# The first heads of an attention stage: rows of maxima on ScalarE's queue, copies and loads in another order, and twelve transposes by transpose mode

## The chip, the cores and the metric

The kernel runs on one core of a Trainium2 chip. The metric is the device time of one execution, in microseconds. The kernel before was timed three times: 921.12, 921.53 and 918.25 us, median 921.12 us.

The core has five engines with instruction queues of their own: TensorE (PE; its weight loads, PEld, run beside it), VectorE (DVE), ScalarE (ACT), GpSimd (POOL) and SyncE (SP). Each works through its instructions in the order in which they are written, and waits where an instruction needs something that is not there yet. A DMA is issued by an engine's queue too: by SP nearly everywhere here, by ACT for the first weights of the last stage and, after the change, for a few small rows.

## The reference

Three stages follow each other: causal attention with a decay, a gated feed-forward network, and eight experts to which tokens are assigned greedily.

```python
# attention: 4 batches x 8 heads = 32 heads, 576 positions, 64 columns
scores = (q @ k.T) / sqrt(64) + cum[:, None] - cum[None, :]   # cum = cumsum(log(clip(f)))
scores = where(causal, -1e9, scores); scores -= max(scores, -1)
attn = exp(scores); attn /= sum(attn) + 1e-9;  x = attn @ v
# gated network on 2304 tokens x 512
x = (sigmoid(x @ w_gate) * (x @ w_val)) @ w_out
# 8 experts, 288 tokens each: the greatest logits of x @ w_gate2 first, until an expert is full
out[mask_e] = maximum(x[mask_e] @ w1[e], 0) @ w2[e]
```

## The kernel before

**What a head needs.** `attention` works on 32 heads, two to a pair. For head h:

- `load(p)` brings q and k of a pair (576 KB) into one of three buffers `raw`; `decays(p)` adds two rows (the decay) to it; `load_v(p)` brings v (`vf`, 330 KB, three buffers).
- `prep(h)` (ACT, L126) rounds q and k into one of four tiles `P1` (`P` in the trace). Row 66 of that tile holds the row of maxima; rows 64 to 66 start as ones, and 64 zero columns stand ahead.
- `copies(h)`: two DMAs of 144 KB from `P1` into the tile `p2` (`p` in the trace). `prep2(h)` (POOL, L139 and L140) fills the other halves of it with the remainders of the rounding.
- `maxpass(h)`: TensorE makes the rounded scores (six matmuls, into `p1b` and `pb`), DVE takes the maxima of the 128-row blocks (L159).
- `mrows(h)`: TensorE turns the maxima into rows (`pb<-identr,mx`), ACT copies them (L185); `mstore(h)` sends them by DMA (2.5 KB, L188) into row 66 of `P1`.
- `scores(h)`: twelve matmuls; the first of them (`py<-P`) needs row 66, the others `p2` too. ACT takes the exponentials (L208), and POOL cuts the diagonal blocks (`affine_select`, L212).
- `av(h)`: TensorE multiplies by `vf` (ten jobs into `pv`), ACT copies the result (L238), and `store` sends a pair's result to DRAM.

**The order.** Nothing is scheduled by a program: the order of each engine is that of the calls. In the loop over h, TensorE does `scores(h)`, then `av(h-1)` with `mrows(h+2)` and `maxpass(h+3)` set between its jobs, so each row of maxima is made about two heads before it is used. The first heads are written out apart: there is not yet a head to lay the work beside, and `warm(n)` fills gaps with n matmuls whose results nobody reads. In the loop, head 1 has `rows(2)`, `prep(4)` and `maxpass(3)`, and head 2 has `mrows(3)` at the end of `scores(2)`, `maxpass(4)`, `rows(4)`, and then `maxpass(5)`.

**Before the loop.** The decay (`ck`) is made by DVE and ACT from f (L111 to L116), and goes by DMA into rows 64 and 65 of `P1` (L130); only then can `maxpass(0)` start. Meanwhile POOL sets the ones and zeros of the four `P1` tiles (L104, L105) and the ones in `raw` (L119).

**Later.** `fill(h)` puts the splitting of the next stage's weights (DMA `mr<-ww`, L406 to L423) beside the heads. After attention come the gated network (`Ffn`), the assignment (`Route`), and `First.turn`: it turns the 288 gathered rows of expert 0 by matmuls with an identity matrix, three for each of four column blocks (L1020), and adds 16 rows that came another way (L1022). The experts turn their rows in the same manner, but with `nc.tensor.transpose` (L1047).

Of the kernel before, what the change touches and what calls it, by code (L numbers as in the profile page):

```python
# [6 lines left out]
F32 = mybir.dt.float32  # L7
# [27 lines left out]
def make_consts(ev, pool, keep):  # L35

    nc = ev.nc

    jp = pool.tile([128, 128], I32, name="jp")
    nc.gpsimd.iota(jp, pattern=[[1, 128]], base=0, channel_multiplier=-1)  # L40
    ev.identb = pool.tile([128, 128], BF16, name="identb")
    nc.vector.tensor_scalar(ev.identb, jp, 0.0, None, op0=OP.is_equal)
    yield
    ev.mq = pool.tile([128, S], BF16, name="mq")
    nc.vector.memset(ev.mq[:, :448], 0.0)
    nc.vector.tensor_scalar(ev.mq[:, 448:], jp, 0.0, BIG, op0=OP.is_gt, op1=OP.mult)
    ev.identr = pool.tile([128, 128], F32R, name="identr")
    nc.vector.tensor_scalar(ev.identr, jp, 0.0, None, op0=OP.is_equal)
    yield
    ev.ident = keep.tile([128, 128], F32, name="ident")  # L50
    nc.vector.tensor_scalar(ev.ident, jp, 0.0, None, op0=OP.is_equal)
    ev.fold = keep.tile([16, E], F32, name="fold")
    nc.vector.tensor_tensor(ev.fold, ev.ident[:16, 0:8], ev.ident[:16, 8:16], op=OP.add)
    yield
# [2 lines left out]

AT = (2, 4)
FIRST = {2: -3, 4: -2, 5: -1}
WARM = (19, 4, 6, 2)  # L60
KT = [(0, 0, 0, 1024), (0, 128, 128, 0), (0, 256, 256, 512), (0, 384, 384, 832), (64, 448, 512, 448)]


def attention(ev, qkT, vr, f, xs, rec, ckd, fill):
# [4 lines left out]
    with ExitStack() as ctx:  # L69
# [11 lines left out]
        def load(p):  # L81
            r = RAW3[p % 3]
            nc.sync.dma_start(r[0:64], qkT[2 * p:2 * p + 2].rearrange("h d s -> d h s"))
            RAW[2 * p], RAW[2 * p + 1] = r[:, 0], r[:, 1]

        def decays(p):

            nc.sync.dma_start(RAW3[p % 3][64:66, :, S:], ckd[:, 2 * p:2 * p + 2])
# [11 lines left out]
        nc.scalar.activation(idle, zero, AF.Ln, bias=1.0)  # L100
        next(consts)
        P1 = [st.tile([67, 64 + 2 * S], F32R, name=f"P1_{i}") for i in range(4)]
        for t in P1:
            nc.gpsimd.memset(t[64:67].bitcast(F32), 1.0)  # L104
            nc.gpsimd.memset(t[0:64, 0:64].bitcast(F32), 0.0)  # L105

        junk = st.tile([128, 1600], BF16, name="mj")
        JT = (0, 64, 256, 576, 1024)
        ck = st.tile([NHEAD, 2, S], F32R, name="ck")
        next(consts)  # L110
        nc.vector.tensor_scalar(ft, ft, 1e-4, 1.0, op0=OP.max, op1=OP.min)  # L111
        nc.scalar.activation(ft, ft, AF.Ln)
        cum = st.tile([NHEAD, S], F32, name="cum")
        nc.vector.tensor_tensor_scan(cum, ft, zero.to_broadcast([NHEAD, S]), 0.0, op0=OP.add, op1=OP.add)
        nc.vector.tensor_scalar(ck[:, 0], cum, -8.0, None, op0=OP.mult)
        nc.vector.scalar_tensor_tensor(ck[:, 1], cum, -8.0, ck[:, 0], op0=OP.mult, op1=OP.subtract)  # L116

        def ones(p):
            nc.gpsimd.memset(RAW3[p][64:66, :, :S], 1.0)  # L119
# [4 lines left out]
        def prep(h, n=66):  # L124
            p1 = P1[h % 4]
            nc.scalar.activation(p1[0:n, Q0:], RAW[h][0:n], AF.Copy)  # L126
            P2[h] = wk.tile([128, 2 * S], F32R, name="p2", bufs=4)

        def decay(h):
            nc.sync.dma_start(P1[h % 4][64:66, K0:].bitcast(F32), ck[h:h + 1].bitcast(F32))  # L130

        def copies(h):
            p1, p2 = P1[h % 4], P2[h]
            nc.sync.dma_start(p2[0:64, :S].bitcast(F32), p1[0:64, Q0:K0].bitcast(F32))
            nc.sync.dma_start(p2[64:128, S:].bitcast(F32), p1[0:64, K0:].bitcast(F32))

        def prep2(h, engine=nc.gpsimd):
            r, p1, p2 = RAW.pop(h), P1[h % 4], P2[h]
            engine.tensor_tensor(p2[64:128, :S], r[0:64, :S], p1[0:64, Q0:K0], op=OP.subtract)  # L139
            engine.tensor_tensor(p2[0:64, S:], r[0:64, S:], p1[0:64, K0:], op=OP.subtract)  # L140
# [44 lines left out]
            nc.scalar.activation(MR[h], b[0:5, 0:128], AF.Copy)  # L185

        def mstore(h):
            nc.sync.dma_start(P1[h % 4][66:67, 0:640].bitcast(F32), MR.pop(h))  # L188

        def scores(h, m=None):  # L190
            p1, p2 = P1[h % 4], P2.pop(h)
            y = ps2.tile([128, 1024], F32, name="py")
            x = ps1.tile([128, 512], F32, name="p1b")
            z = ps1.tile([128, 512], F32, name="p1b")

            def sc(out, k0, q0, q1, first=True, last=True):
                mm(out, p1[0:67, K0 + k0:K0 + k0 + 128], p1[0:67, Q0 + q0:Q0 + q1], first, False)
                mm(out, p2[:, S + k0:S + k0 + 128], p2[:, q0:q1], False, last)

            sc(y[:, 256:512], 0, 0, 256)  # L200
            sc(y[:, 512:832], 0, 256, 576)
            sc(x[:, 0:448], 128, 128, 576, last=False)
            sc(x[:, 448:512], 448, 512, 576, False)
            sc(z[:, 0:320], 256, 256, 576, last=False)
            sc(z[:, 320:512], 384, 384, 576, False)
            e = EX[h] = wk.tile([128, 1600], F32, name="e", bufs=3)
            for c0, c1, src in ((1024, 1600, y[:, 256:832]), (0, 512, x), (512, 1024, z)):
                nc.scalar.activation(e[:, c0:c1], src, AF.Exp, scale=0.125)  # L208

            for first, step, n, base in ((0, 512, 3, 0), (448, 384, 2, 64)):  # L210
                t = blocks(e, first, step, n)
                nc.gpsimd.affine_select(out=t, in_=t, pattern=[[-base, n], [1, 128]], compare_op=OP.is_ge, fill=0.0,  # L212
                                        base=base, channel_multiplier=-1)
            if m:
                mrows(m)
# [46 lines left out]
        warm(WARM[0])  # L262
        for h in (0, 1):
            decay(h)
        nc.sync.dma_start(ckd.rearrange("r h s -> h r s"), ck.bitcast(F32))
        for h in (0, 1):
            prep(h, 64)
# [21 lines left out]
        load_v(0)  # L289
        copies(2)  # L290
        decays(2)
        load(2)
        copies(3)
        warm(WARM[3])
        maxpass(2)
        prep2(3)
        ones(2)
        for h in range(1, NHEAD):
            odd = h % 2
            scores(h, 3 if h == 2 else None)  # L300
            if h == 1:
                ones(0)
            if h == 2:
                mstore(3)
                next(consts)

            def rows(r):
                if r < NHEAD:
                    mrows(r)
                    mstore(r)  # L310

            def early():
                rows(h + 2 if h > 1 else 2)
                if h == 1:
                    prep(4)
                    prep2(4)
                elif h + 4 < NHEAD:
                    prep(h + 4)

            def late():  # L320
                if h + 3 < NHEAD:
                    maxpass(h + 3)

            if h == 1:
                av(0, {2: early, 3: lambda: maxpass(3)})
                prep(5)
            elif h == 2:
                av(1, {0: lambda: maxpass(4), 5: early})
                late()
            else:  # L330
                av(h - 1, {AT[0]: early, AT[1]: late})
            if h < NHEAD - 3:
                copies(h + 3)
            if h >= 3 and odd:
                store(h // 2 - 1)
            if h == 1:
                load(3)
                decays(3)
            if not odd and h // 2 + 3 < NPAIR:
                load(h // 2 + 3)  # L340
                decays(h // 2 + 3)
            if odd and h // 2 + 1 < NPAIR:
                load_v(h // 2 + 1)
            for b in range(B - 1):
                step = {2: 0, 4: 1, 5: 2}.get(h - (b + 1) * H)
                if step is not None:
                    recip(b, step)
            if h + 4 < NHEAD:
                prep2(h + 4)
            if h in FIRST:  # L350
                fill(FIRST[h])
            fill(h)
# [640 lines left out]
class First:  # L993
# [19 lines left out]
    def turn(self, x, bank):  # L1013

        nc = self.nc
        for k in range(4):
            ks = slice(k * 128, (k + 1) * 128)
            p = bank()
            for i in range(3):
                nc.tensor.matmul(p[:, i * TT:(i + 1) * TT], self.xg[i][:, ks], self.ev.ident[:TT, :TT], start=i == 0,  # L1020
                                 stop=False, skip_group_check=True)
            nc.tensor.matmul(p[:, :CH], x[:, ks], self.hot[:, :CH], start=False, stop=True, skip_group_check=True)  # L1022
            nc.scalar.activation(self.x[0][:, k], p[:, :CH], AF.Copy)  # L1023
            nc.vector.tensor_tensor(self.x[1][:, k], p[:, :CH], self.x[0][:, k], op=OP.subtract)  # L1024
# [251 lines left out]
```

## Time and profile before

| what | value |
|---|---|
| runs | 918.25, 921.12, 921.53 us |
| profiled execution: its own time | 924.52 us |
| its span, first to last instruction | 922.6 us |
| mean granted TensorE clock, as a share of full speed | 0.987 |
| PE busy | 901.5 us (98%) |
| DVE, ACT, POOL busy | 548.7, 330.7, 459.9 us |
| the chain that ended last | PE 22%, issue 4%, POOL 2% (within the part that was followed back) |

The span of the profile lies 1.92 us under the execution's own time; the rest is start and end. A busy PE is not a PE at its peak: with the granted clock at one half the same matmuls take twice as long and still count as busy. So the rows of the clock are read beside those of the busy time. The attention stage takes about the first 190 us, the gated network goes on to about 600 us, the assignment to about 676 us, and the experts to the end.

### The profile page before, as it was taken

How to read it: one execution, taken by the hardware profiler on the slowest of the kernel's cores; microseconds unless marked ns; L12 is line 12 of the kernel's file. 1: busy time of each engine (PE TensorE's matmuls, PEld its weight loads, DVE VectorE, ACT ScalarE, POOL GpSimd, SP SyncE). 2: the span in 40 equal slices, each digit the busy share in tenths (PEclk: the TensorE clock that was granted, in tenths of full speed). 3: DMA queues.
4: the chain of work that ended last, by engine and by line, in shares of the span. 5: the costliest groups of instructions: out<-in, count | busy, mean ns of one | idle time of the engine just before them, and what ended most of it. 6: DMA issues, size and time to landing. Idle time of an engine off the chain costs nothing. (4 is left out here: it accounts for less than half of the span.)

```text
span 922.6 us, 14053 instructions
## 1 busy us (share of the span) xinstructions
PE 901.5 (98%) x5182; PEld 758.9 (82%) x5182; DVE 548.7 (59%) x1185; ACT 330.7 (36%) x571; POOL 459.9 (50%) x393
## 2 busy tenths in 40 slices
PE   7899999999999999999999999999989999999995
PEld 4677777778788888888888888887789999999995
DVE  5387886818885497988989642535524443444431
ACT  5566667642322211121111222211126444444530
POOL 8678898925565122121222221222138777777741
PEclk9899999999999999999999999999979999999998
DMA  6777999845551203010121210011247666656610
GB/s 142 164 205 213 237 235 235 213 130 170 171 168 64 75 0 92 18 63 13 47 62 26 66 46 1 1 44 46 70 144 233 207 190 193 196 172 210 201 37 26
DMA packets 49016, 111.30 MB, mean 121 GB/s; under 512 B 11346, under 2 KB 11762, under 8 KB 48946
## 3 DMA queue, kind: packets, MB, share of 16 engines
q1 hardware_dynamic: 44786, 98.85, 37.7%
q0 software_dynamic: 3072, 9.44, 3.1%
q10 hardware_dynamic: 1088, 2.10, 0.7%
q8 instruction: 41, 0.67, 0.3%
q14 instruction: 29, 0.24, 0.1%
HBM read 86.12 MB, written 14.71 MB: 109 GB/s over the span
## 5 line engine op out<-in xcount | busy, mean ns | idle before, releaser
L509 POOL TENSOR_TENSOR gl<-sg,gh 128x512 fp32r<-128x512 f32 x36 | 49.7, 1379 | 201.1 <-ACT gh L508 201.1
L985 POOL TENSOR_TENSOR elo<-eraw,ehi 128x1024 fp32r<-128x1024 f32 x45 | 107.9, 2410 | 45.2 <-ACT ehi L983 44.9
L143 PE MATMUL pv<-e,vf 128*65 128x256 f32 (+1 forms) x434 | 106.5, 370 | 0.8 <-DMA vf<-vv 0.8
L502 PE MATMUL gv<-xah,w_hi 128*128 128x512 f32 (+1 forms) x288 | 103.2, 358 | 0.0
L502 PE MATMUL gv<-xal,w_hi 128*128 128x512 f32 (+1 forms) x288 | 102.9, 357 | 0.0
L502 PE MATMUL gv<-xah,w_lo 128*128 128x512 f32 (+1 forms) x288 | 102.8, 357 | 0.0
L542 DVE CUSTOM_DVE_ANT_0 mb<-mb,bc 128x512 f32<-128x512 f32 x96 | 82.2, 856 | 3.3
L542 DVE CUSTOM_DVE_ANT_0 mb<-mr,bc 128x512 f32<-128x512 f32 x96 | 81.9, 853 | 2.8
L508 ACT ACTIVATE gh<-sg 128x512 fp32r<-128x512 f32 x36 | 22.8, 633 | 156.4 <-PE o L521 84.4
L1072 PE MATMUL ey<-hh,ehi 128*128 128x288 f32 x256 | 78.0, 305 | 0.0
L1072 PE MATMUL ey<-hl,ehi 128*128 128x288 f32 x256 | 76.4, 299 | 0.0
L502 PE MATMUL gv<-xbh,w_hi 128*128 128x512 f32 x192 | 76.1, 396 | 0.0
L502 PE MATMUL gv<-xbl,w_hi 128*128 128x512 f32 x192 | 76.1, 396 | 0.0
L502 PE MATMUL gv<-xbh,w_lo 128*128 128x512 f32 x192 | 76.0, 396 | 0.0
L1072 PE MATMUL ey<-hh,elo 128*128 128x288 f32 x256 | 75.7, 296 | 0.0
L143 PEld LDWEIGHTS pv<-e,vf 128*65 128x65 f32 x434 | 50.3, 139 | 25.1 <-issue 15.4
L143 PE MATMUL p1b<-P 66*128 66x192 f32 (+7 forms) x256 | 66.0, 326 | 3.5 <-DMA P<-ck 1.8
L159 DVE CUSTOM_DVE_ANT_0 mj<-p1b,mq 128x192 bf16<-128x192 f32 (+3 forms) x128 | 46.6, 419 | 37.7 <-PE p1b L143 37.7
L1059 PE MATMUL eh<-xeh,ehi 128*128 128x288 f32 x224 | 67.8, 303 | 0.0
L1059 PE MATMUL eh<-xeh,elo 128*128 128x288 f32 x224 | 66.3, 296 | 0.0
L1059 PE MATMUL eh<-xel,ehi 128*128 128x288 f32 x224 | 66.3, 296 | 0.0
L1062 DVE SCALAR_TENSOR_TENSOR hl<-eh,hh 128x288 fp32r<-128x288 f32 x64 | 29.1, 456 | 62.4 <-ACT hh L1061 62.4
(213 smaller groups left out, 2305.7 us busy)
## 6 DMA issues: line engine op xcount, KB each, us to landing
eraw<-w SPq DMA_DIRECT2D x56, 512.0 KB
mr<-ww SPq DMA_DIRECT2D x26, 512.0 KB
raw<-qk SPq DMA_DIRECT2D x16, 576.0 KB
p<-P SPq DMA_DIRECT2D x64, 144.0 KB
vf<-vv SPq DMA_DIRECT2D x16, 330.0 KB
bc<-ww SPq DMA_DIRECT2D x10, 512.0 KB
xs<-xo SPq DMA_DIRECT2D x16, 292.5 KB
x2d<-mr SPq DMA_DIRECT2D x17, 256.0 KB
```

What stands on the lines that cost most here:

```text
L143: nc.tensor.matmul(out, lhsT, rhs, start=start, stop=stop, skip_group_check=True)
L159: nc.vector.tensor_tensor_reduce(out=junk[:, JT[t]:JT[t] + n], in0=src, in1=ev.mq[:, S - n:], op0=OP.add, op1=OP.min, scale=-1.0, scalar=3 ...
L502: nc.tensor.matmul(p[i][:, :m], w_[:, ws], x_[:, k], start=n == 0, stop=n == 11)
L508: nc.scalar.activation(hi, s, AF.Copy)
L509: nc.gpsimd.tensor_tensor(lo, s, hi, op=OP.subtract)
L542: nc.vector.tensor_tensor_reduce(out=junk, in0=a, in1=self.bc[j], op0=OP.mult, op1=OP.add, scale=1.0, scalar=0.0, accum_out=res)
L985: eng.tensor_tensor(lo, r, hi, op=OP.subtract)
L1059: nc.tensor.matmul(p[:, :CH], w_[:, ws], x_[:, k], start=n == 0, stop=n == 11)
L1062: nc.vector.scalar_tensor_tensor(h[1][:, f], p[:, :CH], 0.0, h[0][:, f], op0=OP.max, op1=OP.subtract)
L1072: nc.tensor.matmul(p[:, :CH], w_[:, ws], h_[:, f], start=n == 0, stop=n == 23)
```

## The change

1. `mstore(h)` issues from ACT's queue for h < 6, and from SP's as before for the others.
2. The ones of `P1` are no longer set by POOL: tiles 0 and 1 by ACT (after the logarithm), tiles 2 and 3 by DVE (after `ck`). POOL keeps the zero columns.
3. The loop's first three heads are written anew: `mrows(3)` and `mstore(3)` stand ahead of `scores(2)`; `prep(4)`, `prep(5)` come behind the exponentials of head 2; `copies(4)` and `copies(5)` with them; `maxpass(4)` behind `av(1)`, and `maxpass(6)` and `rows(5)` behind `av(2)`.
4. `load(3)` and `load_v(1)` are issued before the loop, and `load_v` runs one pair further ahead all through; `copies(3)` goes ahead of `load(2)`.
5. The 128x128 identity and the 16x8 fold matrix are made at heads 30 and 31 and not at head 2; `warm` has 20 matmuls and not 19 at the start.
6. In `First.turn` the three matmuls with the identity carry `is_transpose=True`.

```diff
-WARM = (19, 4, 6, 2)
+WARM = (20, 4, 6, 2)
...
         P1 = [st.tile([67, 64 + 2 * S], F32R, name=f"P1_{i}") for i in range(4)]
-        for t in P1:
-            nc.gpsimd.memset(t[64:67].bitcast(F32), 1.0)
-            nc.gpsimd.memset(t[0:64, 0:64].bitcast(F32), 0.0)
...
         nc.scalar.activation(ft, ft, AF.Ln)
+        for t in P1[:2]:
+            nc.scalar.activation(t[64:67], zero[0:3].to_broadcast([3, 64 + 2 * S]), AF.Copy, bias=1.0)
...
+        for t in P1[2:]:
+            nc.vector.memset(t[64:67].bitcast(F32), 1.0)
...
         def mstore(h):
-            nc.sync.dma_start(P1[h % 4][66:67, 0:640].bitcast(F32), MR.pop(h))
+            (nc.scalar if h < 6 else nc.sync).dma_start(P1[h % 4][66:67, 0:640].bitcast(F32), MR.pop(h))
...
         for h in (0, 1):
             decay(h)
+        for t in P1:
+            nc.gpsimd.memset(t[0:64, 0:64].bitcast(F32), 0.0)
...
         decays(2)
+        copies(3)
         load(2)
-        copies(3)
+        load(3)
+        load_v(1)
...
-            scores(h, 3 if h == 2 else None)
-            if h == 1:
-                ones(0)
             if h == 2:
+                mrows(3)
                 mstore(3)
-                next(consts)
+            scores(h)
...
             if h == 1:
-                av(0, {2: early, 3: lambda: maxpass(3)})
-                prep(5)
+                ones(0)
+                decays(3)
+                av(0, {2: lambda: rows(2), 3: lambda: maxpass(3)})
             elif h == 2:
-                av(1, {0: lambda: maxpass(4), 5: early})
+                prep(4)
+                prep2(4)
+                av(1)
+                prep(5)
+                prep2(5)
+                maxpass(4)
+            elif h == 3:
+                av(2, {2: lambda: rows(4), 3: lambda: maxpass(5), 5: lambda: prep(6)})
+                rows(5)
+                prep(7)
                 late()
+                prep2(6)
             else:
                 av(h - 1, {AT[0]: early, AT[1]: late})
-            if h < NHEAD - 3:
+            if h == 2:
+                copies(4)
+                copies(5)
+            elif 2 < h < NHEAD - 3:
                 copies(h + 3)
...
-            if odd and h // 2 + 1 < NPAIR:
-                load_v(h // 2 + 1)
+            if odd and h > 1 and h // 2 + 2 < NPAIR:
+                load_v(h // 2 + 2)
...
                 nc.tensor.matmul(p[:, i * TT:(i + 1) * TT], self.xg[i][:, ks], self.ev.ident[:TT, :TT], start=i == 0,
-                                 stop=False, skip_group_check=True)
+                                 stop=False, is_transpose=True, skip_group_check=True)
```

**Where instructions moved.** Three places, each before and after. The first is ACT's order from the exponentials of head 1 to those of head 3 (`e<-` exponentials, `mr<-pb` copies of rows of maxima, `P_0_116` and `P_1_117` the tiles that heads 4 and 5 use, `xo<-pv` results of `av`). Before:

```order
L208 ACTIVATE e<-py 128x576
L208 ACTIVATE e<-p1b 128x512 x2
L185 ACTIVATE mr<-pb 5x128
L126 ACTIVATE P_0_116<-raw_105 66x1152
L238 ACTIVATE xo<-pv 65x576
L126 ACTIVATE P_1_117<-raw_105 66x1152
L208 ACTIVATE e<-py 128x576
L208 ACTIVATE e<-p1b 128x512 x2
L185 ACTIVATE mr<-pb 5x128 x2
```

and after, over the same piece of work:

```order
L209 ACTIVATE e<-py 128x576
L209 ACTIVATE e<-p1b 128x512 x2
L186 ACTIVATE mr<-pb 5x128
L189 DMA P_2_118<-mr 1x5x128
L239 ACTIVATE xo<-pv 65x576
L186 ACTIVATE mr<-pb 5x128
L189 DMA P_3_119<-mr 1x5x128
L209 ACTIVATE e<-py 128x576
L209 ACTIVATE e<-p1b 128x512 x2
L127 ACTIVATE P_0_116<-raw_105 66x1152
L239 ACTIVATE xo<-pv 65x576
L127 ACTIVATE P_1_117<-raw_105 66x1152
```

Both stores of rows of maxima are now ACT's own, both stand ahead of the exponentials of head 2, and the two `prep` of heads 4 and 5 stand behind them. The second place is TensorE's order from the end of `av(0)` on (`py<-P_2_118` is the first matmul of `scores(2)`, `p1b<-P_0_116` the first of `maxpass(4)`). Before, the last rows of `scores(2)` and what follows:

```order
L143 MATMUL p1b<-P_2_118 128x192
L143 MATMUL p1b<-p_219 128x192
L143 MATMUL pb<-identr,mx 5x128
L143 MATMUL p1b<-P_0_116 128x192
L143 MATMUL p1b<-P_0_116 128x320
L143 MATMUL p1b<-P_0_116 128x448
L143 MATMUL p1b<-P_0_116 128x64
L143 MATMUL pb<-P_0_116 128x256
L143 MATMUL pb<-P_0_116 128x320
L143 MATMUL pv<-e,vf 65x256
```

and after:

```order
L144 MATMUL p1b<-P_2_118 128x192
L144 MATMUL p1b<-p_220 128x192
L144 MATMUL pv<-e,vf 65x256
L144 MATMUL pv<-e,vf 65x320
L144 MATMUL pv<-e,vf 65x128
L144 MATMUL pv<-e,vf 65x320
L144 MATMUL pv<-e,vf 65x192
L144 MATMUL pv<-e,vf 65x64
L144 MATMUL pv<-e,vf 65x320
L144 MATMUL p1b<-P_0_116 128x192
```

The matmuls of `av(1)` now stand between `scores(2)` and `maxpass(4)`, and the row of maxima of head 3 is made before `scores(2)`. The third place is SP's queue from the decay of pair 2 (`raw_105`) on. Before:

```order
L88 DMA raw_105<-ckd 2x2x576
L83 DMA raw_105<-qk 64x2x1152
L134 DMA p_255<-P_3_119 64x576
L135 DMA p_255<-P_3_119 64x576
L188 DMA P_2_118<-mr 1x5x128
L134 DMA p_315<-P_0_116 64x576
L135 DMA p_315<-P_0_116 64x576
L83 DMA raw_103<-qk 64x2x1152
L88 DMA raw_103<-ckd 2x2x576
L92 DMA vf<-vv 128x660
```

and after:

```order
L89 DMA raw_105<-ckd 2x2x576
L135 DMA p_256<-P_3_119 64x576
L136 DMA p_256<-P_3_119 64x576
L84 DMA raw_105<-qk 64x2x1152
L84 DMA raw_103<-qk 64x2x1152
L93 DMA vf<-vv 128x660
L89 DMA raw_103<-ckd 2x2x576
L135 DMA p_367<-P_0_116 64x576
L136 DMA p_367<-P_0_116 64x576
```

The row of maxima of head 2 (`P_2_118<-mr`) no longer stands behind the load of pair 2 and the copies of head 3, and the load of pair 3 and the second `vf` stand ahead of the copies of head 4.

## Rows read from the trace of the kernel before

**Rows 1.** Stretches: start:end, length, busy (x count) by engine, PEclk, DMA share, GB/s.
```profile
30.00:40.00 10.00, 10.00 (x43) 6.84 (x44) 3.58 (x18) 3.84 (x7) 6.00 (x7) 0.71 0.61 134
...
29.00:30.00 1.00, 1.00 (x5) 0.81 (x4) 0.74 (x5) 0.23 (x2) 0.97 (x1) 0.51 0.30 74
```

**Rows 2.** PE in time: start us, us, what [idle before <- releaser].
```profile
22.80 1.27 PE L143 MATMUL pv<-e,vf 128*65 128x192 f32 x5
25.74 0.39 PE L143 MATMUL py<-P 67*128 67x256 f32 x1 [1.67 <-DMA P<-mr]
...
28.66 1.28 PE L143 MATMUL p1b<-P 66*128 66x192 f32 x4 [0.92 <-ACT e L208]
...
36.87 0.28 PE L143 MATMUL py<-P 67*128 67x256 f32 x1
...
39.34 0.46 PE L143 MATMUL pb<-identr,mx 128*5 128x128 f32 x1
...
40.16 0.91 PE L143 MATMUL p1b<-P 66*128 66x192 f32 x4
...
41.24 1.43 PE L143 MATMUL pv<-e,vf 128*65 128x192 f32 x6
42.27 0.52 PE L143 MATMUL py<-P 67*128 67x256 f32 x1
...
47.83 0.52 PE L143 MATMUL py<-P 67*128 67x256 f32 x1
...
50.73 1.16 PE L143 MATMUL pv<-e,vf 128*65 128x256 f32 x4 [0.83 <-DMA vf<-vv]
```

**Rows 3.** SP's queue in time (and PE's weight load that its first store releases).
```profile
13.13 2.97 SPq L188 DMA_DIRECT2D P<-mr  x2
...
15.01 0.19 PEld L143 LDWEIGHTS py<-P 67*128 67x128 f32 x1 [0.30 <-DMA P<-mr]
...
21.62 0.75 SPq L188 DMA_DIRECT2D P<-mr  x1
...
42.99 0.44 SPq L92 DMA_DIRECT2D vf<-vv  x1
```

**Rows 4.** ACT and its queue in time.
```profile
24.84 1.16 ACT L126 ACTIVATE P<-raw 66x1152 fp32r<-66x1152 f32 x1 [3.28 <-DMA raw<-qk]
...
27.49 0.63 ACT L208 ACTIVATE e<-py 128x576 f32<-128x576 f32 x1
28.02 1.07 ACT L208 ACTIVATE e<-p1b 128x512 f32<-128x512 f32 x2
...
685.91 1.98 ACTq L961 DMA_DIRECT2D eraw<-w  x4
```

**Rows 5.** Instructions of a tile (0 to 60) or line: count, ns min/median/max.
```profile
L188 SPq DMA_DIRECT2D P<-mr x9: 700/747/818, 13.1 to 57.9; - x9
...
L406 DVE TENSOR_SCALAR mb<-mr x26: 414/912/2849, 48.5 to 277.2; 128x512 uint32<-128x512 uint32 x26
```

**Rows 6.** The front, all engines in time.
```profile
2.63 1.10 POOL L104 MEMSET P<- 3x1216 f32 x1
2.70 1.34 DVE L111 TENSOR_SCALAR ft<-ft 32x576 f32<-32x576 f32 x1
...
7.83 1.46 SPq L130 DMA_DIRECT2D P<-ck  x2
...
9.84 0.73 PE L143 MATMUL p1b<-P 66*128 66x192 f32 x4 [1.79 <-DMA P<-ck]
```

**Rows 7.** The chain that ended last: start us, us, what.
```profile
680.09 0.64 PE gv L1020 x6
...
681.39 1.23 PE gv L1020 x6
...
702.09 0.25 PE et L1047 x3
```

**Rows 8.** One more stretch, as in Rows 1: the turn of expert 0.
```profile
680.80:691.00 10.20, 9.21 (x35) 7.91 (x34) 2.01 (x5) 2.08 (x5) 2.77 (x3) 0.51 0.59 178
```

More of the change, by code (lines that the diff above doesn't have):

```diff
@@ L51, in make_consts @@
     nc.vector.tensor_scalar(ev.ident, jp, 0.0, None, op0=OP.is_equal)
+    yield
     ev.fold = keep.tile([16, E], F32, name="fold")
@@ L312, in early @@
             def early():
[L313 to L317, printed above, removed]
+                rows(h + 2)
+                if h + 4 < NHEAD:
                     prep(h + 4)
@@ L324, in attention @@
             if h == 1:
-                av(0, {2: early, 3: lambda: maxpass(3)})
-                prep(5)
-            elif h == 2:
-                av(1, {0: lambda: maxpass(4), 5: early})
+                ones(0)
+                decays(3)
+                av(0, {2: lambda: rows(2), 3: lambda: maxpass(3)})
+            elif h == 2:
+                prep(4)
+                prep2(4)
+                av(1)
+                prep(5)
+                prep2(5)
[4 more added lines that the diff above has]
+                prep(7)
                 late()
+                prep2(6)
             else:
                 av(h - 1, {AT[0]: early, AT[1]: late})
-            if h < NHEAD - 3:
+            if h == 2:
+                copies(4)
+                copies(5)
+            elif 2 < h < NHEAD - 3:
                 copies(h + 3)
@@ L335, in attention @@
                 store(h // 2 - 1)
-            if h == 1:
-                load(3)
-                decays(3)
+            if h == 2:
+                load_v(2)
             if not odd and h // 2 + 3 < NPAIR:
@@ L347, in attention @@
                     recip(b, step)
-            if h + 4 < NHEAD:
+            if 2 < h < NHEAD - 4:
                 prep2(h + 4)
+            if h > NHEAD - 3:
+                next(consts)
             if h in FIRST:
```

## The prediction

> **What bounds the kernel now.** I read the stretches first, then TensorE in time, then what released each of its waits. TensorE is busy 98% of the span, so most of the time can only change by work taken from it; but a busy engine at half clock is not working at its pace. The stretches show this: between 29 and 30 us the granted clock is 0.51, and over 30 to 40 it averages 0.71 [rows 1]. That is the level of 1.2 GHz and not 2.4 for about 6.7 us. Just ahead of it TensorE stood still twice: 1.67 us before `scores(2)` at 25.74, waiting for the DMA of the row of maxima, and 0.92 us before `maxpass(4)` at 28.66, waiting for ScalarE's exponentials [rows 2].
>
> How much is lost there? `av(0)` ends at 22.80 + 1.27 = 24.07 and `scores(4)` starts at 42.27: 18.20 us [rows 2]. In between TensorE does two `scores`, two `av`, three `mrows` and three `maxpass`. A settled head has one of each and takes 47.83 - 42.27 = 5.56; one `mrows` more is 0.46 at most (39.34) and one `maxpass` 41.24 - 40.16 = 1.08 [rows 2]. Two heads and these two make 12.66 us of work, so 18.20 - 12.66 = 5.54 us are lost: 2.59 as standstill, the rest, 2.95, by the clock.
>
> Two smaller losses are seen too: 0.83 us before 50.73, where `av(4)` waits for `vf` [rows 2], and the turn of expert 0, where the clock is again 0.51 for 10.2 us [rows 8]. Elsewhere TensorE has little idle time (922.6 - 901.5 = 21 us in the whole span, of which these waits, the start and the end are the most), so what is gained at the front arrives at the end.
>
> **The change part by part.**
>
> *Row of maxima of head 2.* Now: issued at 21.62, used at 25.74, 4.12 us; the first such row took 15.01 - 13.13 = 1.88 [rows 3]. The difference is what stands before it in SP's queue: the load of pair 2 (576 KB) and the copies of head 3 (288 KB), which `prep(4)` waits for as well, until 24.84 [rows 4]. On ACT's queue nothing is ahead of it. But an issue is not free on ACT: SP takes 0.70 to 0.82 us for each [rows 5], and on ACT the copies and exponentials behind it wait that long. For heads 0 and 1 that puts `prep(2)` and the first exponentials up to 0.75 later, and `maxpass(2)` follows these; I take 0.35 lost. So `mrows(2)` is stored at 21.9 and there at 21.9 + 1.88 = 23.8, `av(0)` and `mrows(3)` end at 24.4 + 0.25, and `scores(2)` starts at about 24.65 with no wait for its row. For the latency the ends are 1.88 and 4.12; I take the lower, as nothing else is on that queue.
>
> *Order of heads 1 to 3.* ACT now has, from 24.65 on: the result of `av(0)` (576 columns, as the first exponential: 0.63), the copy of the row of head 3 (128 columns, about 0.3) and its store (0.75), the exponentials of head 2 (1.6, from 27.49 to 29.09, and a little more for waits), `prep(4)` (1.16) [rows 4, 5]: some 4.65, so `prep(4)` ends at 29.3. TensorE in that time does `scores(2)` and `av(1)` (a head less its `mrows` and `maxpass`: 5.56 - 1.54 = 4.0) and is at 28.7. It waits 0.6 us there for `maxpass(4)`; before, the same place cost 0.92 and the half clock. The load of pair 2 is issued 1.9 later than now, behind the copies of head 3, and what had to be through the queue by 25.7 is about the same; ACT wants it at 28.1, so it is not late. Then `scores(3)` at 30.4 (its row stored at 25.6, there at 27.5), `av(2)` at 32.2 (its `vf` issued at 21.6 behind 1.4 MB, there at about 28 to 30), `maxpass(5)` and `maxpass(6)` with `prep(5)` and `prep(6)` done at 31.1 and 35.5. `scores(4)` comes at 24.4 + 12.66 + 0.6, less the `mrows` pieces that overlap, about 37.3 in place of 42.27. With the 0.35 of the stores already in it this part gives 4.9 us. Ends: 2.6 if all the half-speed time stays, 5.5 if no wait is left.
>
> *`vf` one pair further ahead.* For `av(4)` it was issued at 42.99, 7.7 us ahead of its use at 50.73 [rows 2, 3]; after, it goes out behind the copies of head 5, at about 31, more than 11 us ahead. The 0.83 goes. Ends 0 and 0.83; I take 0.8.
>
> *The front.* `maxpass(0)` waits for `ck`: DMA issued 7.83, first matmul 9.84 [rows 6]. L111 on DVE takes 1.34 us beside a POOL memset of 1.10 [rows 6]; the same kind of operation over 512 columns takes between 0.41 and 2.85 [rows 5], so what stands beside it decides. With four of POOL's memsets gone, `ck` is between 0 and 1.2 us earlier; I take 0.8, and half of it survives the waits behind it: 0.4. The ones by ACT cost two passes of about 1.2 us (1152 columns take 1.16 [rows 4]), behind which `prep(0)` comes 0.5 later; its users (`prep2(0)`, the copies) are needed at 15.01 [rows 3], so this is covered; were it not, 0.5 is the price. The ones by DVE, some 2.6 us, just fit ahead of the first maxima. One more `warm` matmul and the identity at heads 30 and 31 (DVE) lie beside waits or idle time: nothing. Ends of this part: -0.8 and +1.2.
>
> *The transposes.* Each matmul with the identity runs as two passes now (six for three blocks): 0.64 us at full clock, 1.23 at half, and there are two of the latter [rows 7]. Of the four column blocks the first is hidden by a wait, so 0.64 + 1.23 + 1.23 = 3.10 lie on the path. Three real transposes take 0.25 at full clock [rows 7], 0.5 at half: 1.25 left, 1.85 gained. If the clock comes back at the same moment as now, only the full-speed worth of it is gained, three times 0.39 = 1.2. I take 1.2. Ends: -0.5 (TensorE has less to do there, and the half clock of [rows 8] lasts longer) and 1.9.
>
> Sum: 4.9 + 0.8 + 0.4 + 1.2 = 7.3 us. The profiled execution took 924.5, so like for like 917.2. The median of the runs is 921.1, 3.4 below it; I apply the sum there: 913.8, and say 914.0.
>
> **Rivals.**
>
> *The row comes no sooner (A).* All transfers may share what really delays the row, whatever queue issues it: it would again take 4.12 us and be there at 26.0, 1.4 us after TensorE is ready, and at `scores(4)` 0.4 late. The sum falls by 1.8 to 5.5: 915.6; if the standstill of 1.4 brings the half clock again, as 1.67 did, the 2.95 go too: 918.6. For it: DMA engines are 61% busy there [rows 1]. Against: 1.88 us with only copies ahead [rows 3]. The Trainium skill states a rule for this (DMA: Bandwidth & Descriptors, Issuing engines are not separate DMA queues): DMAs of different engines run on the same 16 DMA engines and interleave, and another issuing engine saves only the issue time. Read strictly, that is this rival; but interleaving is just what a small row behind 864 KB lacks, and no run here shows which holds.
>
> *The loss is the profiled execution's own (B).* It took 3.4 us more than the median. If the other executions do not have the 6.7 us at half clock, what is left to gain is smaller by about 3.3: 917.3. For it: that difference. Against: the two standstills come from the order and would be in every run.
>
> *ACT is held until its row has landed (C), slower.* If a store on ACT's queue kept that engine for the whole 1.88 and not 0.75 us, six stores would cost 6 x 1.13 = 6.8 us of ACT, all of it on the path between 13 and 37 us, where `prep`, exponentials and rows take turns; each is a standstill like those before 25.74, and the half clock (3.3) stays. 921.1 - 7.3 + 6.8 + 3.3 = 923.9. It decides from about 1.9 us per store. Against: four issues of 512 KB each pass ACT's queue in 1.98 us [rows 4], which cannot be their landing.
>
> **How the numbers follow.** Forecast 0.68, with 910 to 917; A 0.13 (915.6 to 918.6); B 0.12 (917.3); C 0.07 (923.9). Less than 0.5% (4.6 us) cannot be told from no change here, so faster means under 916.5, slower over 925.7. Of the forecast 0.64 lie under 916.5, of A 0.06, of B 0.03: 0.73 faster. Slower: half of C and a remainder for unseen things such as a longer half clock in the first 20 us, 0.06. Same: 0.21. The range takes in A and B and both ends of the front: 909.8 to 918.8; C is left out.
>
> **What would show it.** In the changed profile: `scores(2)` starts near 24.7 with no wait for the row of maxima; the wait before `maxpass(4)` is under 1 us and names `prep`; the granted clock stays 1.00 from 20 to 40 us; `scores(4)` starts at 36.5 to 38; no wait for `vf` later; L1020 has 12 matmuls, and the stretch at 0.51 after 680 begins about 6 us earlier and is no longer than 10.2. I am wrong if the clock still falls before 40 us, or if ACT shows pauses over 1 us behind each store.

## The result, and the profile after

The changed kernel is slower: 932.26 us (median of 4, 931.01 to 932.70) against 921.33 before (4 runs, 918.25 to 922.56). The medians differ by 10.9 us; the ratio of the runs is 1.0114, with a 95% interval of [1.0079, 1.0148]. I forecast 914.0. The profiled execution took 932.7 us (span 930.8, granted clock 0.981). Line numbers after are one higher in most of `attention` and fifteen higher in the turn of expert 0; in the experiments they differ by a few more.

TensorE in time, where it waits or starts a `scores` (start us, us, what, [idle before <- releaser]); these answer to [rows 2, 6]:

```profile
10.00 0.72 PE L144 MATMUL p1b<-P 66*128 66x192 f32 x4 [2.46 <-DMA P<-ck]
...
17.13 0.52 PE L144 MATMUL py<-P 67*128 67x256 f32 x1
20.86 0.28 PE L144 MATMUL py<-P 67*128 67x256 f32 x1
32.51 0.58 PE L144 MATMUL py<-P 67*128 67x256 f32 x1 [5.83 <-DMA P<-mr]
41.01 0.28 PE L144 MATMUL py<-P 67*128 67x256 f32 x1
...
50.05 0.58 PE L144 MATMUL py<-P 67*128 67x256 f32 x1 [1.82 <-DMA P<-mr]
58.11 0.52 PE L144 MATMUL py<-P 67*128 67x256 f32 x1
```

The six lines of `py` are `scores(0)` to `scores(5)`. The steps between them say where the time went (before: 25.74 to 47.83 [rows 2], and `scores(1)` in the same view:)

```profile
18.32 0.28 PE L143 MATMUL py<-P 67*128 67x256 f32 x1
```

| step | before | after | difference |
|---|---|---|---|
| start to `scores(1)` | 18.32 | 20.86 | +2.54 |
| to `scores(2)` | 7.42 | 11.65 | +4.23 |
| to `scores(3)` | 11.13 | 8.50 | -2.63 |
| to `scores(4)` | 5.40 | 9.04 | +3.64 |
| to `scores(5)` | 5.56 | 8.06 | +2.50 |

That is +10.28 by `scores(5)`. The two spans differ by 8.2: the turn of expert 0 was shorter in this execution than in the one shown of before, which itself lay 3.4 us over its median. The row that was to come without a wait is now waited for 5.83 us, and the next pair's first row 1.82. The stretches (start:end, length, busy of PE, PEclk, DMA share, GB/s) show what lies around the waits; they answer to [rows 1]:

```profile
12.00:18.00 6.00, 5.64 (x19) 0.50 0.44 114
...
26.00:28.00 2.00, 0.68 (x3) 1.00 1.06 213
28.00:30.00 2.00, 0.00 (x0) 0.60 1.01 194
30.00:32.00 2.00, 0.00 (x0) 0.50 0.62 126
32.00:34.00 2.00, 1.49 (x5) 0.50 0.01 5
28.00:39.00 11.00, 6.49 (x21) 0.53 0.32 64
48.00:56.00 8.00, 6.18 (x23) 0.57 0.88 268
```

At head 2 TensorE stands still while the DMA engines are full, and starts just after they have gone empty. At head 4 (50.05) they stay full past its start. Behind each of the three standstills (front, head 2, head 4) the granted clock is 0.50, the lower level, for several us. SyncE's queue in time shows what was issued ahead of the row (answering to [rows 3]):

```profile
21.19 0.46 SPq L135 DMA_DIRECT2D p<-P  x1
21.70 0.60 SPq L136 DMA_DIRECT2D p<-P  x1
22.34 1.39 SPq L84 DMA_DIRECT2D raw<-qk  x2
23.78 0.59 SPq L93 DMA_DIRECT2D vf<-vv  x1
```
ScalarE and its queue, in time, have the row itself (answering to [rows 4]):
```profile
24.07 0.70 ACTq L189 DMA_DIRECT2D P<-mr  x1
26.64 0.65 ACT L239 ACTIVATE xo<-pv 65x576 f32<-65x576 f32 x1 [2.60 <-PE pv L144]
...
33.87 0.65 ACT L209 ACTIVATE e<-py 128x576 f32<-128x576 f32 x1 [6.44 <-PE py L144]
```

The row of head 2 goes out at 24.07, behind copies of head 3 (2 x 144 KB), loads of pairs 2 and 3 (2 x 576 KB) and `vf` (330 KB): 1770 KB in 2.9 us. It is used 8.44 us later. ScalarE itself was held 0.70 us and then waited for TensorE, not for its row. The turn of expert 0 has three real transposes per block, 0.25 us at full clock as expected, 0.48 at half (the chain, answering to [rows 7]):

```profile
691.95 0.48 PE gv L1035 x3
...
694.54 0.25 PE gv L1035 x3
```

### The profile page after: what moved, and what is told of

The parts are those of the page before. It is cut to its first block, busy times and chain, and to the rows that moved or that the text cites. A ratio compares the mean times of both kernels' runs of the same rounds, so it can differ in the third digit from the quotient of the medians.

```text
span 930.8 us, 14049 instructions
## 1 busy us (share of the span) xinstructions
PE 903.7 (97%) x5171; PEld 759.3 (82%) x5171; DVE 547.3 (59%) x1187; ACT 334.1 (36%) x573; POOL 455.8 (49%) x389
## 5 line engine op out<-in xcount | busy, mean ns | idle before, releaser
L998 ACT ACTIVATE ehi<-eraw 128x1024 fp32r<-128x1024 f32 x60 | 63.3, 1055 | 5.7 <-DMA eraw<-w 5.6
```

The source lines that it names most:

```text
L998: nc.scalar.activation(hi, r, AF.Copy)
```

## The experiments

Theory **T1**: a row lands about when the bulk that was issued before it has drained, whichever queue issued either; the loss comes from the load of pair 3 and `vf` of pair 1 put ahead of the row of head 2 (and their like ahead of head 4's). Rival **T2**: ScalarE's queue is served late. Ratios are to the kernel before, run on the same chip beside the experiments; its medians there were 921.2, 921.2 and 921.4.

**Rows back on SyncE's queue.**
```
-            (nc.scalar if h < 6 else nc.sync).dma_start(P1[h % 4][66:67, ...
+            nc.sync.dma_start(P1[h % 4][66:67, ...
```


> The changed kernel with one part undone: all rows of maxima are stored by SyncE's queue again, behind the load of pairs 2 and 3 and vf of pair 1. Theory T1 (a row lands when the bulk that was issued before it has drained, whichever queue issued either): the row of head 2 lands as late as now, scores(2) starts between 31.5 and 33 us with over 5 us of wait for the row, and the time stays at 930 to 933 us. Theory T2 (it is ScalarE's queue that is served late): the row comes about 4.1 us after its issue as in the kernel before, scores(2) starts near 28, and the time falls to 921 to 926.


Measured 931.45 us, 1.0101 [1.0081, 1.0121]: as slow as with ScalarE's queue. TensorE waits 5.77 us for the row of head 2 (issued 21.82) and 5.43 for head 4's:
```profile
29.44 0.58 PE L144 MATMUL py<-P 67*128 67x256 f32 x1 [5.77 <-DMA P<-mr]
...
51.27 0.58 PE L144 MATMUL py<-P 67*128 67x256 f32 x1 [5.43 <-DMA P<-mr]
```
`scores(2)` at 29.44 is earlier than T1 said because the bulk went out 3 us earlier as well (from 18.20); issue to use is 7.62 us. T2 falls.

The equal times of the two kernels are put together from unlike parts in the two executions shown. This one has no half clock in the front (`scores(1)` at 17.86 in place of 20.86) and loses more at head 4. There the row (issued 43.67) stands on SyncE's queue behind two loads of the next stage's weights (2 x 512 KB, from 42.74). In the changed kernel the row goes out on ScalarE's queue at 44.28, ahead of them (45.10), and is waited for 1.82 us.

**Rows on ScalarE's queue, pair 3's load and `vf` on it too, behind the row.**
```
-        load(3)
-        load_v(1)
...
-                av(0, {2: lambda: rows(2), 3: ...
+                av(0, {2: lambda: (rows(2), load(3, nc.scalar), load_v(1, nc.scalar)), 3: ...
```


> The changed kernel with the rows still on ScalarE's queue, but the load of pair 3 and vf of pair 1 issued on ScalarE's queue too, right behind the row of head 2, so that only the copies of head 3 and the load of pair 2 are under way when the row goes out. T1: the row lands about 4.1 us after its issue in place of 8.4, scores(2) starts at 28 to 29 in place of 32.5; ScalarE pays about 1.3 us for the two issues; the time is 926 to 930. T2: the row still takes some 8 us, scores(2) starts at 32 or later, 932 to 935.


Measured 922.37 us, 1.0028 [1.0003, 1.0053]: 9.9 us below the changed kernel by the medians (7.9 by the ratios), more than expected. ScalarE's queue shows row, load and `vf` in their new order:
```profile
21.94 0.70 ACTq L189 DMA_DIRECT2D P<-mr  x1
22.73 1.17 ACTq L84 DMA_DIRECT2D raw<-qk  x1
23.94 0.93 ACTq L93 DMA_DIRECT2D vf<-vv  x1
```
TensorE at `scores(2)`:
```profile
26.63 0.39 PE L144 MATMUL py<-P 67*128 67x256 f32 x1 [2.08 <-DMA P<-mr]
```
The stretch in which the row lands (columns as above):
```profile
26.00:27.00 1.00, 0.37 (x3) 1.00 1.12 267
```
`scores(2)` starts 1.4 us ahead of T1's 28 to 29, since the row goes out 2.13 us earlier than in the changed kernel. Issue to use is 4.69 us, and the engines are still full with the bulk that went out behind the row: the row did not wait for all of that. The clock is 1.00 from 8 to 40 us in this execution, in the front too. The changed kernel had half clock in both places, so more was gained than the wait; how much of it belongs to the front, no run separates.

**Rows on SyncE's queue, pair 3's load and `vf` behind the row there.**
```
-        load(3)
-        load_v(1)
...
-                decays(3)
                 av(0, {2: lambda: rows(2), 3: lambda: maxpass(3)})
+                load(3)
+                load_v(1)
+                decays(3)
```


> The changed kernel with rows on SyncE's queue and the load of pair 3 and vf of pair 1 put behind the row of head 2 in that queue, as in the kernel before. T1: the row lands 4 to 4.5 us after its issue, scores(2) starts at 27.5 to 29, and the time is 924 to 928, well below the kernel that has only its rows on SyncE's queue. T2: no difference to that kernel.


Measured 927.17 us, 1.0064 [1.0041, 1.0086], 4.3 under the first experiment. The row of head 2 takes 3.91 us (21.54 to 25.45, T1 said 4 to 4.5); head 4's, with `vf` of pair 2, the load of pair 4 and 2 x 512 KB of weights still ahead, costs 4.47 us of waiting at 42.77.

**All bulk behind the rows of heads 2 and 4, which are on SyncE's queue.**
```
-        load(2)
-        load(3)
-        load_v(1)
...
                 av(0, {2: lambda: rows(2), 3: lambda: maxpass(3)})
+                load(2)
+                load(3)
+                load_v(1)
+                decays(3)
...
-                av(2, {2: lambda: rows(4), 3: ...
+                av(2, {2: lambda: (rows(4), load_v(2), load(4), decays(4)), 3: ...
...
```


> The changed kernel with rows on SyncE's queue and all bulk behind them: the loads of pairs 2 and 3 and vf of pair 1 go out behind the row of head 2, vf of pair 2 and the load of pair 4 behind the row of head 4. T1: the row of head 2 lands 1.9 to 2.5 us after its issue, scores(2) starts at 25.5 to 27 with a wait under 1 us, and scores(4) has no wait for its row; the next wait is ScalarE's for the load of pair 2, which now goes out at about 24 and lands near 28, so maxpass(4) waits 1 to 2 us: 921 to 926. T2: rows as fast as in the kernel that has only its rows on SyncE's queue, and a time at or above its, since the loads are later.


Measured 919.75 us, 0.9984 [0.9962, 1.0006], below T1's range. TensorE:
```profile
23.85 0.33 PE L144 MATMUL py<-P 67*128 67x256 f32 x1
32.35 0.39 PE L144 MATMUL py<-P 67*128 67x256 f32 x1 [1.83 <-DMA P<-mr]
```
The lines are `scores(2)` and `scores(3)`. There is no wait at `scores(2)` or `scores(4)`. The row of head 3, now behind that bulk (1482 KB), is the late one: 7.55 us from its issue at 24.80.

**Before, with rows on ScalarE's queue alone.**
```
-            nc.sync.dma_start(P1[h % 4][66:67, ...
+            (nc.scalar if h < 6 else nc.sync).dma_start(P1[h % 4][66:67, ...
```


> The kernel before with only the rows of maxima of heads 0 to 5 moved to ScalarE's queue; the bulk ahead of the row of head 2 (load of pair 2, copies of head 3) stays as it is on SyncE's queue. T1 (a row lands when the bulk issued before it has drained): it lands 3.5 to 4.5 us after its issue, as before on SyncE's queue, scores(2) at 25.5 to 26.5, and the time is 920 to 923. The prediction's own step (nothing is ahead of it on ScalarE's queue): 1.9 us and scores(2) near 24.6, 915 to 919. T2 (ScalarE's queue is served late): 7 us or more, scores(2) near 29, 925 or more.


Measured 918.97 us, 0.9975 [0.9955, 0.9994]. `scores(2)` starts at 24.72 without a wait, 2.13 us after the row's issue at 22.59 on ScalarE's queue:
```profile
22.59 0.70 ACTq L188 DMA_DIRECT2D P<-mr  x1
...
24.72 0.53 PE L143 MATMUL py<-P 67*128 67x256 f32 x1
```
That is what the prediction said, not T1's number. But the stretches (columns as above) show that the engines were nearly empty by then:
```profile
20.00:22.00 2.00, 2.00 (x14) 1.00 1.04 245
22.00:24.00 2.00, 2.00 (x14) 1.00 0.56 114
24.00:26.00 2.00, 2.00 (x14) 1.00 0.02 4
```
With no rows to wait for, SyncE issued the load of pair 2 at 17.52 in place of 18.32. This run alone doesn't tell overtaking from an empty queue; the next does.

**The same, with pair 3's load and `vf` ahead of the row.**
```
         load(2)
         copies(3)
+        load(3)
+        load_v(1)
...
             if h == 1:
-                load(3)
                 decays(3)
...
-            if odd and h // 2 + 1 < NPAIR:
+            if odd and h > 1 and h // 2 + 1 < NPAIR:
```


> The kernel before with its own order of work, rows of heads 0 to 5 on ScalarE's queue, and only the load of pair 3 and vf of pair 1 issued ahead of the row of head 2. T1: the row of head 2, whose wait was under 0.3 us without the two loads ahead, now lands only when all of it has drained, scores(2) starts at 27.5 to 30 in place of 24.7, the clock falls behind it, and the time is 923 to 928 where the same kernel without the two loads ahead took 919.0. The rival (the changed order of heads 1 to 3 loses the time, not the loads): 918 to 920.


Measured 923.13 us, 1.0017 [0.9997, 1.0037], 4.2 us above the kernel in which the two loads come later (by the medians; 3.9 by the ratios). On SyncE's queue the two loads go out:
```profile
21.26 0.65 SPq L83 DMA_DIRECT2D raw<-qk  x1
21.95 0.61 SPq L92 DMA_DIRECT2D vf<-vv  x1
```
On ScalarE's queue the row follows:
```profile
22.91 0.70 ACTq L188 DMA_DIRECT2D P<-mr  x1
```
TensorE waits for it:
```profile
28.87 0.39 PE L143 MATMUL py<-P 67*128 67x256 f32 x1 [3.43 <-DMA P<-mr]
```
The stretches around that wait:
```profile
26.00:28.00 2.00, 0.00 (x0) 1.00 1.01 259
28.00:30.00 2.00, 1.13 (x8) 1.00 0.25 61
30.00:36.00 6.00, 6.00 (x21) 0.50 0.88 205
```
Order of work and queue are as in the kernel above; the row takes 5.96 us in place of at most 2.13, lands as the engines empty, and half clock follows. T1 holds for this row.

**Before, with the transposes alone.**
```
-                                 stop=False, skip_group_check=True)
+                                 stop=False, is_transpose=True, skip_group_check=True)
```


> The kernel before with only the real transposes in the turn of expert 0. If their gain is what the changed kernel's trace shows (from the first gv matmul to the first et matmul of expert 1 36.95 us in place of 41.0), the time falls by 2 to 4 us, to 917 to 919. The rival, that less work there only makes the half clock last or fall elsewhere, gives 920 to 922, with a stretch at half clock or a wait for hl further on.


Measured 921.77 us, 1.0008 [0.9991, 1.0026]: no gain. The trace of before had half clock for 10.2 us in the turn [rows 8]; other executions have less, or none. The 36.95 against 41.0 us of the expectation run from TensorE's first wait in the turn to `et<-ident,y` (L1082, the turning of expert 0's results; the expectation names expert 1). With plain matmuls at full clock, in the kernel before with rows on ScalarE's queue, that way takes 36.92 us (675.63 to 712.55). So the difference was the clock of the execution shown of before.

**Before, with the front alone** (ones, zeros, one more warm-up matmul).
```
-WARM = (19, 4, 6, 2)
+WARM = (20, 4, 6, 2)
...
-            nc.gpsimd.memset(t[64:67].bitcast(F32), 1.0)
...
+        for t in P1[:2]:
+            nc.scalar.activation(t[64:67], zero[0:3].to_broadcast([3, 64 + 2 * S]), AF.Copy, bias=1.0)
...
+        for t in P1[2:]:
+            nc.vector.memset(t[64:67].bitcast(F32), 1.0)
```


> The kernel before with only the front changed: ones by ScalarE and VectorE, GpSimd's zeros later, one more warm-up matmul. The prediction's term says 0.4 us gained: 920 to 921.5. The rival from the changed kernel's trace (ck is issued earlier but lands no sooner, so the standstill before maxpass(0) grows from 1.8 to 2.5 us and the clock falls for 6 us) says 1 to 2 us lost: 922 to 924; with the fall seen in some executions only, a spread wider than the kernel before has.


Measured 920.67 us, 0.9994 [0.9978, 1.001]. `ck` is issued at 6.60, `maxpass(0)` starts at 9.73 after 1.12 us of waiting, at full clock.

**Each bulk transfer behind a row.** From the kernel with all bulk behind: the load of pair 2 stays behind the row of head 2, the load of pair 3 and `vf` of pair 1 move behind that of head 3.
```
             if h == 2:
                 mrows(3)
                 mstore(3)
+                load(3)
+                load_v(1)
+                decays(3)
...
-                av(0, {2: lambda: rows(2), 3: lambda: maxpass(3)})
-                load(2)
-                load(3)
-                load_v(1)
-                decays(3)
+                av(0, {2: lambda: (rows(2), load(2)), 3: lambda: maxpass(3)})
```


> The changed kernel with rows on SyncE's queue and each bulk transfer behind a row that would otherwise wait for it: the load of pair 2 behind the row of head 2, the load of pair 3 and vf of pair 1 behind the row of head 3, vf of pair 2 and the load of pair 4 behind the row of head 4. T1: rows of heads 2, 3 and 4 are waited for less than 0.5 us each, the granted clock stays at 1.00 from 20 to 50 us, and the 1.83 us and the half clock that the kernel with all bulk behind the row of head 2 still has at scores(3) go: 914.5 to 917.5. The rival, that standstills move to the late loads (prep(6) or vf): 918 to 921.


Measured 916.28 us, 0.9945 [0.9927, 0.9964]. No row is waited for; 0.97 us for `vf` before `av(2)` is left, with half clock behind it. The profiled execution had the front's standstill (2.08 us, then clock 0.50 from 14 to 18).

**28 warm-up matmuls on top of it.**
```
-WARM = (20, 4, 6, 2)
+WARM = (28, 4, 6, 2)
```


> The kernel with each bulk transfer behind a row (rows on SyncE's queue), with 28 warm-up matmuls at the start in place of 20, so that TensorE works until ck has landed. If the half clock between 11 and 18 us in some executions comes from the standstill before maxpass(0), it is gone in the profile and in every run: granted clock 1.00 there, scores(0) at 14.9 to 15.2, 914.5 to 916.5 and a narrower spread. The rival, that the longer warm-up holds maxpass(0) back by as much as it saves: no difference, or 0.5 us slower.


Measured 917.11 us, 0.9952 [0.9927, 0.9977]: the wait and the half clock in the front are gone from the profile (`scores(0)` at 14.86), the time is not lower, and lies above the expected 914.5 to 916.5. Its turn of expert 0 is the one to read for the transposes, since the clock is 1.00 there. From TensorE's first wait in it to the start of expert 0, and the wait that comes later:
```profile
673.63 0.30 PE L1032 MATMUL gv<-ident,mr 96*128 96x96 f32 x1 [0.87 <-DMA mr<-x2d,idx]
...
678.82 0.40 PE L1071 MATMUL eh<-xe0h,ehi 128*128 128x288 f32 x1 [0.99 <-DVE xe0l L1036]
...
692.85 0.40 PE L1071 MATMUL eh<-xe0h,ehi 128*128 128x288 f32 x1 [2.17 <-DVE hl L1074]
```
The same turn with plain matmuls, also at 1.00, in the kernel before with rows on ScalarE's queue:
```profile
675.63 0.46 PE L1020 MATMUL gv<-ident,mr 96*128 96x96 f32 x2 [0.56 <-DMA mr<-x2d,idx]
...
682.06 0.40 PE L1059 MATMUL eh<-xe0h,ehi 128*128 128x288 f32 x1 [0.99 <-DVE xe0l L1024]
...
693.70 0.40 PE L1059 MATMUL eh<-xe0h,ehi 128*128 128x288 f32 x1 [0.18 <-DVE hl L1062]
```
5.19 us against 6.43: 1.24 saved, and then 2.17 us of waiting for `hl` where the plain matmuls have 0.18. VectorE spent 3.11 us on a split of expert weights, and `hl` came behind it (ScalarE's part of these splits waits for the weights' DMA, 0.86 us before the one at 686.92). VectorE in time, in the kernel with 28 warm-up matmuls:
```profile
689.32 3.11 DVE L997 TENSOR_TENSOR elo<-eraw,ehi 128x1024 fp32r<-128x1024 f32 x1 [0.55 <-ACT ehi L995]
692.35 1.17 DVE L1074 SCALAR_TENSOR_TENSOR hl<-eh,hh 128x288 fp32r<-128x288 f32 x3
```

**`vf` of pair 1 ahead of the load of pair 3**, with 28 warm-up matmuls too.
```
                 mstore(3)
-                load(3)
                 load_v(1)
+                load(3)
```


> As the kernel with 28 warm-up matmuls, and vf of pair 1 ahead of the load of pair 3 behind the row of head 3. T1 (transfers land in the order in which they were issued): the wait for vf before av(2), 0.97 us in the kernel with each bulk behind its row, goes, scores(4) starts near 38 to 39 in place of 42, and the time is 912.5 to 915. The rival: the load of pair 3 comes 1.7 us later and prep(6) and maxpass(6) wait for it instead: 915 to 917.


Measured 914.84 us, 0.9939 [0.9915, 0.9964], the lowest median of all and faster than both kernels. The first line is `scores(2)`, the other two are `scores(3)` and `scores(4)`:
```profile
23.45 0.33 PE L144 MATMUL py<-P 67*128 67x256 f32 x1
29.32 0.76 PE L144 MATMUL p1b<-P 66*128 66x192 f32 x4 [0.99 <-ACT P L127]
30.26 0.28 PE L144 MATMUL py<-P 67*128 67x256 f32 x1
...
38.96 0.28 PE L144 MATMUL py<-P 67*128 67x256 f32 x1
```
What is left is 0.99 us for `prep(4)`, and half clock behind that. By the program `prep(4)` needs the load of pair 2; the profile puts ScalarE's wait ahead of it down to `vf`. The median is just inside T1's range; the interval overlaps those of the two kernels around it, so the swap alone isn't shown to gain.

**`vf` of pair 1 behind the load of pair 2**, otherwise as the last.
```
-                av(0, {2: lambda: (rows(2), load(2)), 3: ...
+                av(0, {2: lambda: (rows(2), load(2), load_v(1)), 3: ...
...
-                load_v(1)
                 load(3)
```


> As the kernel with 28 warm-up matmuls, with vf of pair 1 right behind the load of pair 2, so behind the row of head 2 and ahead of the row of head 3. T1: no wait for vf before av(2); the row of head 3 has 330 KB more ahead of it and lands some 1.5 us later, which scores(3) just bears or waits up to 0.5 us for: 912.5 to 915.5. The rival, that the wait for vf is merely turned into one for the row of head 3 of 1 us or more with a half clock behind it: 916 to 919.


Measured 917.42 us, 0.9949 [0.9924, 0.9974]: not distinguishable from the last three. No row is waited for, `scores(4)` comes at 37.95, and the median is in the rival's range without the wait that the rival named.

## Why the prediction was wrong

**The step that failed** is the landing of the row of head 2: "On ACT's queue nothing is ahead of it. ... For the latency the ends are 1.88 and 4.12; I take the lower". It took 8.44, outside both ends. I saw that the load of pair 2 and the copies were ahead of it on SyncE's queue, and took a queue of its own for a way past them. And I wrote that what had to be through "is about the same", though the change puts 906 KB more (load of pair 3 and `vf`) in front. I counted those transfers only for their own users, not for the row behind them.

The trace of before already spoke against the step. These are its stretches around the landing of that row, which is used at 25.74 [rows 2] (columns as in [rows 1]):
```profile
23.00:24.00 1.00, 1.00 (x5) 0.38 (x4) 1.00 (x7) 0.00 (x0) 0.87 (x3) 1.00 0.89 173
24.00:25.00 1.00, 0.07 (x1) 0.00 (x0) 0.16 (x2) 0.16 (x1) 1.00 (x1) 1.00 0.57 119
25.00:26.00 1.00, 0.26 (x2) 0.26 (x3) 0.00 (x0) 1.00 (x2) 0.00 (x0) 1.00 0.07 16
```
The row landed as the DMA engines ran empty (0.89, 0.57, 0.07). The 61% that I weighed for rival A are the share between 30 and 40 us, where this row no longer waits.

- *Which bulk is ahead decides.* Issue to first use of this row: 8.44 us behind 1770 KB (after, ScalarE's queue) and 7.62 (the same bulk, SyncE's queue); 5.96 with the two loads added to the kernel before; 4.12 behind 864 KB (before) [rows 2, 3]; 4.69 and 3.91 with the two loads behind it; at most 2.40 with all bulk behind it. By the medians, taking the two loads from in front of the row gave 9.9 us with rows on ScalarE's queue and 4.3 on SyncE's; adding them to the order of before cost 4.2. By the ratios it is 7.9, 3.4 and 3.9.
- *Rival A was right that another queue brings this row no sooner, and wrong in size.* It kept the 4.12 us of before, so it ended at 918.6 at most and still forecast a gain. The Trainium skill's rule (DMA: Bandwidth & Descriptors, Issuing engines are not separate DMA queues) says that another issuing engine saves only the issue. The runs agree as far as they go: 1.0101 and 1.0114 with either queue.
- *The new order of heads 1 to 3* was worth something: in the last three experiments, with the bulk behind the rows and 28 warm-up matmuls, `scores(4)` comes at 37.95 to 38.96 where I said 37.3. Before it was 42.27 in the execution shown, and 41.24 and 41.47 in the two experiments that keep the order of before and its rows on SyncE's queue. In the changed kernel only the step to `scores(3)` shows it (-2.63).
- *`vf` one pair further ahead* took its own wait away (0.83 us before `av(4)` [rows 2], none in the changed kernel), but the first such load is 330 of the 906 KB in front of the row.
- *The front* got its `ck` issued 1.2 us earlier (6.63 against 7.83), but `maxpass(0)` started 0.16 later: between 8 and 10 us the DMA engines were still 0.65 busy (before 0.15). In the experiments with this front and 20 warm-up matmuls it starts between 9.36 and 9.79, against 9.84 before. The term (0.4 us) lies within the interval of the run of its own (0.9994 [0.9978, 1.001]), and so does no gain at all. In the profiled execution the longer standstill was followed by half clock, the +2.5 of the first step. Two of the four runs have a mean clock of 0.987, not 0.981, and are only about 1 us shorter.
- *The transposes* saved 1.24 us where the clock is alike, as predicted (1.2), and nothing in the time. In the kernel with 28 warm-up matmuls the wait for `hl` behind them takes it back (2.17 us against 0.18). In the trace of the transposes alone no such wait is seen; there half clock makes the turn 6.74 us long, against 6.43 with plain matmuls at full clock. So what takes the gain differs between executions, and one cause for all is not shown. I had looked at the turn and not at what limits expert 0.
- *Rival B* was partly right: the profiled execution of before was 924.5 us at a mean clock of 0.987, and many of its later runs lie at 0.990 to 0.994. The long half clock in its turn was not typical.
- *Rival C* is refuted: 0.69 to 0.71 us per store on ScalarE, 1.29 for the first.

Still open: by what mechanism inside the DMA engines a 2.5 KB row waits for bulk, and how much of the delay comes from bulk that is issued after it on another queue (the row of head 3 in the kernel before with ScalarE's rows took 6.17 us, 28.53 to 34.70, with copies, a load and `vf`, 1482 KB in all, issued in the 3.5 us ahead of it and another load 0.7 us behind it, and it landed with the engines still full, 1.03 between 34 and 35 us).

## What to carry to other kernels

Before moving a small transfer that the path waits for, add up the bytes issued in the microseconds ahead of it on every queue: here they decided when it landed, and a queue of its own brought it no sooner past bulk that was already issued (8.44 us against 7.62). It can only get ahead of bulk that another queue has not issued yet, as the row of head 4 did (1.82 us of waiting against 5.43). In-order waiting on one queue can be useful: SyncE's wait for a row holds later loads back, and a row moved to another queue lets them run ahead (the load of pair 2 at 17.52 in place of 18.32). And compare the same stretch in several executions before pricing a gain by its clock.

## What was not expected of the hardware

A standstill of TensorE does not by itself bring the lower clock: 2.08 us before `scores(2)` with the two loads on ScalarE's queue left it at 1.00, 2.08 us before `maxpass(0)` in another kernel was followed by 0.50, and so was 3.43 us before 28.87. An elementwise pass of VectorE over 576 columns took 0.45 us with GpSimd's memsets gone, 1.34 beside one [rows 6].
